# A written order of operations for the opening of an attention and mixing kernel, with 64-bit weights rounded by an integer add

## The chip, the cores and the metric

The kernel runs on one core of a Trainium2 chip. The metric is the device time of one execution in microseconds (us), lower is better. Engines: PE does matmuls (TensorE) and PEld loads their weights, DVE is VectorE, ACT is ScalarE, POOL is GpSimd, SP issues the DMAs.

## What is computed

Three layers in a row, over 4 batches of 768 tokens: local attention with 8 heads of 64, a token-mixing layer, and a gated layer. The opening of the kernel does attention and the first half of the mixing layer for batch 0:

```python
# attention, per chunk of 32 tokens: 8 memory keys and 16 + 32 + 8 keys around the chunk
a = softmax(scale * q_c @ k_full.T);  out_c = a @ v_full
# mixing layer
theta = x @ w_theta
zr, zi = x * cos(theta), x * sin(theta)
y = einsum('ts,bsd->btd', w_tok_r, zr) + einsum('ts,bsd->btd', w_tok_i, zi)
u = x + y
x2 = u + max(u @ w_ch, 0)
# gated layer: h = gelu(x2 @ w_in); u, v = halves; v normalised, mixed over tokens by w_sg, + b_sg
out = x2 + (u * v_s) @ w_out
```

`w_theta`, `w_tok`, `w_ch`, `w_in` and `w_out` come as 64-bit floats, everything else as 32-bit floats.

## The kernel before

Every product of the mixing layer is made of three fp32r matmuls: each operand is split into a high part `hi` (the value rounded to fp32r, written by ACT) and a rest `lo` (value minus `hi`, by DVE), and hi x hi, hi x lo and lo x hi are added up in PSUM.

*Attention* goes in blocks i of 128 tokens, six to a batch. `att_s` (S): 64 small matmuls give the scores, DVE takes the maximum (L255) and subtracts it (L257), ACT does exp (L261). `att_t` (T): four transposes on PE (L269), copied out by ACT (L273). `att_v` (V): 64 small matmuls (L244), DVE makes the reciprocal of the sums (L281, L284) and multiplies (L285); that is x. `att_x` (X): four transposes of x (L296), split into `xhi` (ACT, L122) and `xlo` (DVE, L123). S and V share one PSUM tile, T and X another.

*Units.* The mixing layer's work is a list of units. For batch 0 there are twelve, one for each half of the output tokens and each of six token blocks s; from unit 12 on a unit covers both halves and half of the channels. `theta(n)` is 12 matmuls (L323; 512 columns wide for batch 0, 256 later), then on DVE a rounding step to the nearest integer (L334) and a subtraction (L337), on ACT sine, absolute value and cosine, and on DVE the multiplication by x that gives z (L348). `z_split` makes the hi and lo of z. `mix_group(n, g)` is six matmuls of 384 columns (L390); the last token block adds x to the sum (L400, L401) and stores it (L402).

*Weights.* A 64-bit piece is brought to fp32 by bit operations on its two words: `bits` (ACT reads the high word, L160; DVE shifts it, L163, sets the sign, L166, and makes a power of two out of the exponent, L170). `convert` then has ACT write `hi` (L213) and DVE compute the low word's share (L214), value minus `hi` (L218) and their sum (L219). The four `w_theta` pieces and the first two of the twelve `w_tok` pieces go through `convert_pe`, which lets PE add the parts by matmuls with an identity.

*Order.* Before the loop a list of calls starts blocks 0 to 3; the loop over units then places attention steps and weight conversions by fixed distances (`s_it`, `x_it`). Within what depends on what, the framework's scheduler reorders instructions. `keep_warm` issues matmuls on a constant whose result is not used. SP issues all DMAs in program order; a load waits until its room is free.

Of the kernel before, what the change touches and what calls it, by code (L numbers as in the profile page):

```python
# [18 lines left out]
DM = H * D  # L19
# [12 lines left out]


def net_kernel(tc, qt, kw, vw, ident, w_theta, w_tok, w_ch, w_in, w_sg, w_out, g_ln, b_sg, out):
# [27 lines left out]
    st_cm, stg = opened("stg", bufs=2)  # L62
# [5 lines left out]
    id_th = stg.tile([128, 128], F32, name="id_th", bufs=1)  # L68
    id_r = stg.tile([128, 128], F32R, name="id_r", bufs=1)
    id_neg = stg.tile([128, 128], F32R, name="id_neg", bufs=1)  # L70
# [19 lines left out]
    def x_set(pool, i, xt):  # L90
        return (
            xt,
            pool.tile([128, KD, S], F32R, name=f"xhi{i}"),
            pool.tile([128, KD, S], F32R, name=f"xlo{i}"),
        )

    sets = {0: x_set(set0, 0, [set0.tile([128, DM], F32, name=f"xt{s}") for s in range(NBLK)])}
    xt_of = [sets[0][0], [None] * NBLK]
# [7 lines left out]

    def keep_warm(bank, n):

        for _ in range(n):
            nc.tensor.matmul(  # L110
                out=bank, lhsT=busy, rhs=busy.unsqueeze(1).to_broadcast([128, 4, 128]),
                start=True, stop=True,
            )
# [7 lines left out]
    def split(hi, lo, src, eng=None):  # L121
        nc.scalar.activation(out=hi, in_=src, func=AF.Copy)  # L122
        (eng or nc.vector).tensor_tensor(out=lo, in0=src, in1=r32(hi), op=ALU.subtract)  # L123

    class Weights:
# [28 lines left out]
        def bits(self, raw, n, scale, mag="act", rem="dve"):  # L154
# [4 lines left out]
            m = self.pool.tile([128, self.n], I32, tag="cvm", name="cvm", bufs=self.ncm)[:, 0:n]  # L159
            nc.scalar.activation(  # L160
                out=h.bitcast(F32), in_=high.bitcast(F32), func=AF.Copy, scale=REBIAS
            )
            nc.vector.tensor_scalar(  # L163
                out=h, in0=h, scalar1=3, scalar2=None, op0=ALU.logical_shift_left
            )
            nc.vector.scalar_tensor_tensor(  # L166
                out=h, in0=high, scalar=-0x80000000, in1=h,
                op0=ALU.bitwise_and, op1=ALU.bitwise_or,
            )
            nc.vector.tensor_scalar(  # L170
                out=m, in0=h, scalar1=-0x800000, scalar2=None, op0=ALU.bitwise_and
            )
            return high, low, h, m

        def convert_pe(self, j, scale=None, bank=None):

            if j >= len(self.pieces):
                return
            _, hi, lo = self.pieces[j]
            raw, n, _ = self.raw.pop(j)  # L180
            one = 1.0 if scale is None else scale
            high, low, h, m = self.bits(raw, n, scale)

            w, rest = h.bitcast(F32), lo
            nc.scalar.activation(out=hi, in_=w, func=AF.Copy, scale=one)
            nc.vector.scalar_tensor_tensor(
                out=rest, in0=low.bitcast(U32), scalar=one * 2.0 ** -52, in1=m.bitcast(F32),
                op0=ALU.mult, op1=ALU.mult,
            )
            step = n if n <= 512 else n // 2  # L190
            for c in range(0, n, step):
                cv = (bank or th_tile)()[:, 0:step]
                c = slice(c, c + step)
                nc.tensor.matmul(
                    out=cv, lhsT=id_sb if scale is None else id_th, rhs=w[:, c],
                    start=True, stop=False,
                )
                nc.tensor.matmul(out=cv, lhsT=id_neg, rhs=hi[:, c], start=False, stop=False)
                nc.tensor.matmul(out=cv, lhsT=id_r, rhs=rest[:, c], start=False, stop=True)
                nc.scalar.activation(out=lo[:, c], in_=cv, func=AF.Copy)  # L200

        def convert(self, j, mag="act", rem="dve", sub="dve", add="dve"):
            if j >= len(self.pieces):
                return
            eng = {"dve": nc.vector, "pool": nc.gpsimd}
            _, hi, lo = self.pieces[j]
            raw, n, wide = self.raw.pop(j)
            if not wide:
                split(hi, lo, raw[:, 0:n].bitcast(F32), eng[sub])
                return  # L210
            high, low, h, m = self.bits(raw, n, None)
            w, rest = h.bitcast(F32), m.bitcast(F32)
            nc.scalar.activation(out=hi, in_=w, func=AF.Copy)  # L213
            nc.vector.scalar_tensor_tensor(  # L214
                out=rest, in0=low.bitcast(U32), scalar=2.0 ** -52, in1=rest,
                op0=ALU.mult, op1=ALU.mult,
            )
            eng[sub].tensor_tensor(out=w, in0=w, in1=r32(hi), op=ALU.subtract)  # L218
            eng[add].tensor_tensor(out=lo, in0=w, in1=rest, op=ALU.add)  # L219
# [6 lines left out]

    def load_att(i):
        q = at.tile([128, NPAIR, 128], F32, tag="q", name="q", bufs=NQ)
        nc.sync.dma_start(out=q, in_=qt[i].rearrange("p (a t) -> p a t", a=NPAIR))
        q_t[i] = q  # L230
        nc.sync.dma_start(out=ka[i % NK], in_=kw[i])
# [3 lines left out]

# [16 lines left out]
    def att_s(i):  # L252
        sc = pairs(at2_tile(), NKEY, q_t.pop(i), ka[i % NK])
        mx = at.tile([128, 2, NPAIR], F32, tag="mx", name="mx")
        nc.vector.tensor_reduce(out=mx, in_=sc, axis=AX.X, op=ALU.max)  # L255
        p = at.tile([128, NPAIR, 2, NKEY], F32, tag="p", name="p", bufs=1)
        nc.vector.tensor_tensor(  # L257
            out=p.rearrange("p a j k -> p j a k"), in0=sc,
            in1=mx.unsqueeze(3).to_broadcast([128, 2, NPAIR, NKEY]), op=ALU.subtract,
        )  # L260
        nc.scalar.activation(out=p, in_=p, func=AF.Exp, scale=SCALE)  # L261
        p_t[i] = p

    def att_t(i, warm=0):
        p = p_t.pop(i).rearrange("p a j k -> p (a j k)")
        tp = at_tile()
        keep_warm(tp, warm)
        for a in range(NPAIR):
            nc.tensor.transpose(  # L269
                out=tp[:, 128 * a:128 * a + 128], in_=p[:, 128 * a:128 * a + 128], identity=id_sb  # L270
            )
        pt = at.tile([128, NPAIR, 128], F32, tag="pt", name="pt", bufs=1)
        nc.scalar.activation(out=pt, in_=tp.rearrange("p (a t) -> p a t", a=NPAIR), func=AF.Copy)  # L273
        pt_t[i] = pt

    def att_v(i):
        b, s = divmod(i, NBLK)
        x = xt_of[b % 2][s]
        pv = pairs(at2_tile(), D + 1, pt_t.pop(i), va[i % NKV])
        rs = at.tile([128, 2, NPAIR, 1], F32, tag="rs", name="rs")  # L280
        nc.vector.tensor_scalar(  # L281
            out=rs, in0=pv[:, :, :, D:D + 1], scalar1=1e-9, scalar2=None, op0=ALU.add
        )
        nc.vector.reciprocal(out=rs, in_=rs)  # L284
        nc.vector.tensor_tensor(  # L285
            out=x.rearrange("p (a j d) -> p j a d", a=NPAIR, j=2),
            in0=pv[:, :, :, 0:D], in1=rs.to_broadcast([128, 2, NPAIR, D]), op=ALU.mult,
        )

    def att_x(i, warm=0):  # L290
        b, s = divmod(i, NBLK)
        x, (_, xhi, xlo) = xt_of[b % 2], sets[b % 2]
        tp = at_tile()
        keep_warm(tp, warm)
# [784 lines left out]
```

## Time and profile before

| | us |
|---|---|
| median of 3 runs | 745.52 (745.11 to 746.04) |
| the profiled execution | 747.1 |
| its span, first to last instruction | 745.3 |
| PE busy in the span | 727.9 |
| DVE busy | 524.7 |
| ACT busy | 319.0 |

Busy times are unions over an engine's instructions. Matmuls are pipelined, and the end of one is modelled, so the duration that is listed for a matmul is longer than the distance to the next. The granted clock is given as a share of TensorE's full 2.4 GHz; its other level is half of that. A line number can be that of a helper (L122 and L123 are `split`).

### The profile page before, as it was taken

Reading aid. Unit: us, or ns where it says so; the run is one execution under the profiler, and the core shown is the slowest. Engines: PE = TensorE matmul, PEld = TensorE weight load, DVE = VectorE, ACT = ScalarE, POOL = GpSimd, SP = SyncE. Lnnn points to the kernel's source line nnn. Section 1 sums busy time; section 2 is a strip of 40 time slices with the busy share of each in tenths; the row PEclk is TensorE's granted clock in tenths of the full one; section 3 lists DMA queues with packets and bytes.
Section 4 is the critical chain, followed back from the end, with each engine's and each line's share of the span. In section 5 each row is a group of like instructions: output and inputs, shape, how many; then the busy total and the mean of one; then the engine's idle time right before and its main releaser. Section 6 shows DMA issues by size and latency. Waiting matters only on the chain.

```text
span 745.3 us, 16147 instructions
## 1 busy us (share of the span) xinstructions
PE 727.9 (98%) x6958; PEld 672.3 (90%) x6958; DVE 524.7 (70%) x981; ACT 319.0 (43%) x482; POOL 0.3 (0%) x6
## 2 busy tenths in 40 slices
PE   8988999999999999999999999999999999999997
PEld 4766888989999999999999998999899989998997
DVE  5989898757657575799449967977446743774375
ACT  5867543635555455463213516622342233224320
POOL 0000000000000000000000000000000000000000
PEclk9998999999999999999999999999999999999999
DMA  9865465523334240061049936003100310030002
GB/s 350 303 212 176 157 209 165 185 73 122 98 112 127 89 157 31 33 226 69 1 172 352 306 130 246 1 1 106 65 1 1 116 54 1 1 116 11 1 1 85
DMA packets 33047, 86.89 MB, mean 117 GB/s; under 512 B 3792, under 2 KB 16208, under 8 KB 32976
## 3 DMA queue, kind: packets, MB, share of 16 engines
q1 hardware_dynamic: 32976, 85.87, 33.8%
q8 instruction: 54, 0.88, 0.5%
q14 instruction: 17, 0.14, 0.1%
HBM read 66.98 MB, written 18.87 MB: 115 GB/s over the span
## 4 chain that ended last, share of the span: by engine, by line
PE 77%; DVE 14%; ACT 5%; DMA 2%; issue 1%; SPq 0%; ACTq 0%; DVEq 0%
PE acc L390 19%; PE acc L676 13%; PE acc L444 9%; PE th L323 8%; PE acc L552 7%; PE acc L590 7%; PE att L714 6%; PE att L244 3%; DVE z L348 1%; DVE cvh L166 1%; ACT L339 1%; PE att L269 1%; PE th L714 1%; PE acc L714 1%; PE att L296 1%
## 5 line engine op out<-in xcount | busy, mean ns | idle before, releaser
L390 PE MATMUL acc<-tok,slot 128*128 128x384 f32 x552 | 116.9, 342 | 2.2 <-ACT slot L360 2.2
L390 PE MATMUL acc<-slot 128*128 128x384 f32 x552 | 115.3, 339 | 0.0
L390 PEld LDWEIGHTS acc<-tok,slot 128*128 128x128 f32 x552 | 94.5, 188 | 4.6 <-ACT slot L360 2.7
L390 PEld LDWEIGHTS acc<-slot 128*128 128x128 f32 x552 | 95.5, 188 | 1.7
L676 PE MATMUL acc<-sg_hi,vhi_all 128*128 128x384 f32 x192 | 64.6, 336 | 0.8 <-ACT vhi_all L122 0.8
L676 PE MATMUL acc<-sg_lo,vhi_all 128*128 128x384 f32 x192 | 64.4, 336 | 0.0
L676 PE MATMUL acc<-sg_hi,vlo_all 128*128 128x384 f32 x192 | 64.3, 336 | 0.0
L323 PE MATMUL th<-th_hi,xhi 128*128 128x256 f32 (+1 forms) x168 | 52.8, 314 | 1.7 <-ACT xhi L122 1.6
L323 PE MATMUL th<-th_hi,xlo 128*128 128x256 f32 (+1 forms) x168 | 51.6, 307 | 0.3 <-DVE xlo L123 0.3
L323 PE MATMUL th<-th_lo,xhi 128*128 128x256 f32 (+1 forms) x168 | 50.7, 302 | 0.0
L122 ACT ACTIVATE gop<-gv_all 128x384 fp32r<-128x384 f32 (+1 forms) x28 | 15.9, 571 | 76.7 <-DVE gv_all L685 51.6
L681 DVE SCALAR_TENSOR_TENSOR gv_all<-acc,g_col,b_bc 128x384 f32<-128x384 f32 x32 | 19.6, 614 | 41.0 <-PE acc L676 41.0
L590 PE MATMUL acc<-x3lo,in_hi 128*128 128x384 f32 x128 | 43.0, 336 | 0.0
L590 PE MATMUL acc<-x3hi,in_hi 128*128 128x384 f32 x128 | 43.0, 336 | 0.0
L590 PE MATMUL acc<-x3hi,in_lo 128*128 128x384 f32 x128 | 43.0, 336 | 0.0
L444 PE MATMUL acc<-ulo,ch_hi 128*128 128x384 f32 x128 | 42.8, 334 | 0.0
L444 PE MATMUL acc<-uhi,ch_hi 128*128 128x384 f32 x128 | 42.8, 334 | 0.0
L444 PE MATMUL acc<-uhi,ch_lo 128*128 128x384 f32 x128 | 42.8, 334 | 0.0
L559 DVE BATCH_NORM_STATS2 bn<-gv_all 128x6 f32<-128x512 f32 x24 | 16.6, 694 | 33.2 <-ACT gv_all L558 33.2
L552 PE MATMUL acc<-in_hi,x3lo 128*128 128x512 f32 x96 | 38.0, 396 | 0.0
L552 PE MATMUL acc<-in_lo,x3hi 128*128 128x512 f32 x96 | 38.0, 396 | 0.0
L552 PE MATMUL acc<-in_hi,x3hi 128*128 128x512 f32 x96 | 38.0, 395 | 0.0
(186 smaller groups left out, 1574.1 us busy)
## 6 DMA issues: line engine op xcount, KB each, us to landing
va<-vw SPq DMA_DIRECT2D x24, 520.0 KB, 3.8
ka<-kw SPq DMA_DIRECT2D x24, 512.0 KB, 4.7
raw<-w_tok SPq DMA_DIRECT2D x12, 768.0 KB, 5.3
q<-qt SPq DMA_DIRECT2D x24, 256.0 KB, 3.7
u_dram<-u SPq DMA_DIRECT2D x32, 192.0 KB, 1.9
uf<-u_dram SPq DMA_DIRECT2D x8, 768.0 KB, 6.6
x_dram<-x2e SPq DMA_DIRECT2D x32, 192.0 KB, 3.6
x3f<-x_dram SPq DMA_DIRECT2D x8, 768.0 KB, 4.9
```

What stands on the lines that cost most here:

```text
L122: nc.scalar.activation(out=hi, in_=src, func=AF.Copy)
L166: nc.vector.scalar_tensor_tensor(out=h, in0=high, scalar=-0x80000000, in1=h, op0=ALU.bitwise_and, op1=ALU.bitwise_or,)
L244: nc.tensor.matmul(out=out[32 * c:32 * c + 32, j, n * a:n * a + n], lhsT=lhs[h, a, 32 * c:32 * c + 32], rhs=rhs[h, 4 * a + c, :], start=Tr ...
L323: nc.tensor.matmul(out=th, lhsT=a[:, k, tok], rhs=w[:, k, cols], start=(i == 0), stop=(i == 3 * KD - 1),)
L390: nc.tensor.matmul(out=acc[:, 0:TC], lhsT=z[ri][:, zc], rhs=w[:, ri], start=(first and i == 0), stop=(last and i == 5),)
L444: nc.tensor.matmul(out=acc[:, 0:TC], lhsT=w[:, k, ee], rhs=x[:, k, :], start=(i == 0), stop=(i == 3 * KD - 1),)
L552: nc.tensor.matmul(out=acc, lhsT=x[:, k, tt], rhs=w[:, k, :], start=(i == 0), stop=(i == 3 * KD - 1),)
L559: nc.vector.bn_stats(out=p3["bn"][s], in_=gv)
L590: nc.tensor.matmul(out=acc[:, 0:TC], lhsT=w[:, k, ff], rhs=x[:, k, :], start=(i == 0), stop=(i == 3 * KD - 1),)
L676: nc.tensor.matmul(out=acc[:, 0:TC], lhsT=v, rhs=w, start=(i == 0), stop=(i == 3 * NBLK - 1))
L681: nc.vector.scalar_tensor_tensor(out=g, in0=acc[:, 0:TC], scalar=p3["g"][:, f:f + 1], in1=p3["b"][:, tt], op0=ALU.mult, op1=ALU.add,)
L714: nc.tensor.matmul(out=bank, lhsT=wt[:, k, ee], rhs=xt[:, k, :], start=(fresh and i == 0), stop=(i == 5), skip_group_check=not fresh,)
```

## The change

The opening, up to the theta step of unit 13, is written as one list of words, `OPENING`, worked off under `tc.manual_schedule()`, in which the instructions of each engine stay in the order of the list. A word names one operation of one engine and its numbers: S, m, p, e, T, t, V, r, x, X, h, l are attention's steps, A.n.k a quarter (later a half) of theta's matmuls, `ac`, `af`, `as`, `aa`, `ak`, `z` the steps to z, `zh` and `zl` its split, M a mix group, `u` and `us` the addition and the store, `th`- and `tk`-words the seven steps of a conversion of `w_theta` or `w_tok`, `wt` and `wm` the loads of the pieces, W.n n warm-up matmuls. The rest of the loop begins at unit 12 and is scheduled as before.

Three operations change. (1) A 64-bit weight is rounded by an integer add: ACT reads the low word scaled to the range 0 to 8 into an integer (L906), DVE adds it to the shifted bits (L925), and the piece is then split like any value; no piece uses PE. This holds for `w_ch`, `w_in` and `w_out` too. (2) Theta's rounding step is done by ACT, which adds the magic number while it copies out of PSUM (L375); DVE does the rest in one operation (L380). This holds for all units. (3) The hi and lo of the second x set lie in three rooms of the raw pieces of `w_tok` and in one of the conversion's, instead of in a pool that is opened when the conversion's pool is closed.

```diff
+OPENING = """
+k.0 wt.1 q.0 id wt.0 wt.3 k.1 v.0 v.1 q.1 wt.2 wm.0 wm.1 thH.1 wm.4 ths.1 thR.1 thg.1 W.16 S.0 tha.1
...
+"""
...
+    def x_tile(b, j, h):
+        if (b % 2, j, h) not in sets:
+            tag = "cv0" if j and h else "raw"
+            t = sta.tile([128, 4 * TC], F32R, tag=tag, name=tag, bufs=1 if j and h else NRAW1)
...
+    def single(high, low, h, r):
+        nc.scalar.activation(
+            out=h.bitcast(F32), in_=high.bitcast(F32), func=AF.Copy, scale=REBIAS
+        )
+        nc.scalar.activation(out=r, in_=low.bitcast(U32), func=AF.Copy, scale=2.0 ** -29)
+        nc.vector.tensor_scalar(
+            out=h, in0=h, scalar1=3, scalar2=None, op0=ALU.logical_shift_left
+        )
+        nc.vector.scalar_tensor_tensor(
+            out=h, in0=high, scalar=-0x80000000, in1=h, op0=ALU.bitwise_and, op1=ALU.bitwise_or
+        )
+        nc.vector.tensor_tensor(out=h, in0=h, in1=r, op=ALU.add)
+        return h.bitcast(F32)
...
-            nc.vector.scalar_tensor_tensor(
-                out=rest, in0=low.bitcast(U32), scalar=2.0 ** -52, in1=rest,
-                op0=ALU.mult, op1=ALU.mult,
-            )
...
-            eng[sub].tensor_tensor(out=w, in0=w, in1=r32(hi), op=ALU.subtract)
-            eng[add].tensor_tensor(out=lo, in0=w, in1=rest, op=ALU.add)
...
-        nc.vector.tensor_scalar(
-            out=t, in0=th, scalar1=MAGIC, scalar2=MAGIC, op0=ALU.add, op1=ALU.subtract
-        )
-        nc.vector.tensor_tensor(out=t, in0=th, in1=t, op=ALU.subtract)
...
+        nc.scalar.activation(out=t, in_=tmp["th", n], func=AF.Copy, bias=MAGIC)
...
+        nc.vector.scalar_tensor_tensor(
+            out=t, in0=t, scalar=MAGIC, in1=tmp.pop(("th", n)), op0=ALU.subtract, op1=ALU.subtract
+        )
...
+        with tc.manual_schedule():
+            for word in OPENING.split():
+                name, *at_ = word.split(".")
+                step[name](*map(int, at_))
+        close(sb_cm)
+        for it in range(NFIRST, NU):
```

How the instructions stand, first on DVE in the middle of the opening, before: weight pieces 3 and 4 (`cvh`, `cvm`) between attention (`att`, `mx`, `p`, `xlo`) and theta (`th`, `t`).

```order
L166 SCALAR_TENSOR_TENSOR cvh<-raw,cvh 128x768
L257 TENSOR_TENSOR p<-att_609,mx 128x2x4x64
L123 TENSOR_TENSOR xlo_122<-att,xhi_121 128x4x128
L170 TENSOR_SCALAR cvm<-cvh 128x768
L163 TENSOR_SCALAR cvh<-cvh 128x768
L214 SCALAR_TENSOR_TENSOR cvm<-raw,cvm 128x768
L255 TENSOR_REDUCE mx<-att_671 128x8
L218 TENSOR_TENSOR cvh<-cvh,tok_3_109 128x768
L257 TENSOR_TENSOR p<-att_671,mx 128x2x4x64
L334 TENSOR_SCALAR t<-th 128x512
L219 TENSOR_TENSOR tok_3_110<-cvh,cvm 128x768
```

And after, also on DVE, one whole piece (number 4, in tile `cv_710`) between attention, theta (L380), and the split of a z (L446).

```order
L912 TENSOR_SCALAR cv_710<-cv_710 128x768
L254 TENSOR_REDUCE mx<-att_714 128x8
L380 SCALAR_TENSOR_TENSOR t<-t,th 128x512
L259 TENSOR_TENSOR p<-att_714,mx 128x2x4x64
L324 TENSOR_TENSOR xlo_116<-att,xhi_115 128x4x128
L446 TENSOR_TENSOR slot<-z,slot 128x512
L918 SCALAR_TENSOR_TENSOR cv_710<-raw,cv_710 128x768
L446 TENSOR_TENSOR slot_x<-z,slot 128x512
L925 ISA cv_710<-cv_710 128x1536
L411 TENSOR_TENSOR z<-z,xt_119 128x1024
L949 TENSOR_TENSOR tok_4_112<-cv_710,tok_4_111 128x768
```

A piece has four operations instead of six; the add (L925) is issued as an instruction over half-words, 1536 for 768 words.

On PE, late in the opening, before: V of block 7 (`va`), T of block 8 (`p`), mix groups, S of block 9 (`ka`).

```order
L390 MATMUL acc<-slot 128x384 x5
L390 MATMUL acc<-slot,slot_x 128x384
L244 MATMUL att_1479<-va_126,pt 32x65 x32
L269 MATMUL att<-id_sb,p 128x128 x4
L390 MATMUL acc<-slot 128x384 x5
L390 MATMUL acc<-slot,slot_x 128x384
L390 MATMUL acc<-slot 128x384 x5
L390 MATMUL acc<-slot,slot_x 128x384
L244 MATMUL att_1545<-ka_124,q 32x64 x32
```

And after, V of block 7, a mix group, S of block 8, X of block 7.

```order
L273 MATMUL att<-id_sb,p 128x128 x4
L466 MATMUL acc<-slot 128x384 x5
L466 MATMUL acc<-slot,slot_x 128x384
L241 MATMUL att_1386<-va_126,pt 32x65 x32
L466 MATMUL acc<-slot 128x384 x5
L466 MATMUL acc<-slot,slot_x 128x384
L241 MATMUL att_1433<-ka_123,q 32x64 x32
L311 MATMUL att<-id_sb,slot_x 128x128 x4
```

Between a V and the S that takes over its PSUM tile stood two mix groups and a T in this place; now one mix group stands there.

## Rows read from the trace of the kernel before

**Rows 1.** Stretches: length, then busy (instructions) PE, PEld, DVE, ACT, POOL; clock; DMA
```profile
0.00:38.60 38.60, 36.34 (x447) 22.15 (x448) 28.63 (x50) 25.69 (x41) 0.33 (x6) 1.00 0.84 316
38.60:57.50 18.90, 15.42 (x341) 12.07 (x346) 17.14 (x29) 13.15 (x18) 0.00 (x0) 1.00 0.66 224
57.50:65.00 7.50, 6.08 (x78) 4.52 (x63) 6.43 (x9) 5.69 (x8) 0.00 (x0) 0.54 0.64 216
65.00:141.90 76.90, 73.62 (x1245) 64.67 (x1244) 70.15 (x121) 39.15 (x55) 0.00 (x0) 1.00 0.55 175
141.90:745.30 603.40, 596.41 (x4877) 568.92 (x4876) 402.34 (x774) 235.28 (x364) 0.00 (x0) 1.00 0.27 92
```
**Rows 2.** Timeline of PE, end of the opening: start us, us, engine, line, operation
```profile
138.81 1.03 PE L390 MATMUL acc<-slot 128*128 128x384 f32 x5
139.68 0.34 PE L390 MATMUL acc<-slot,slot_x 128*128 128x384 f32 x1
139.86 0.60 PE L296 MATMUL att<-id_sb,slot_x 128*128 128x128 f32 x4
140.21 1.31 PE L390 MATMUL acc<-tok,slot 128*128 128x384 f32 x6
...
141.89 0.86 PE L244 MATMUL att<-ka,q 64*32 64x64 f32 x64
142.68 0.80 PE L390 MATMUL acc<-slot 128*128 128x384 f32 x3
...
144.60 0.69 PE L390 MATMUL acc<-slot 128*128 128x384 f32 x3
```
**Rows 3.** Timeline of ACT and PE, the first 40 us
```profile
7.22 0.68 ACT L160 ACTIVATE cvh<-slot 128x512 f32<-128x512 f32 x1 [5.22 <-DMA slot<-w_theta]
...
20.95 0.39 PE L323 MATMUL th<-th_hi,xhi 128*128 128x512 f32 x1
...
23.52 0.40 PE L323 MATMUL th<-th_hi,xlo 128*128 128x512 f32 x1
...
35.95 0.34 PE L390 MATMUL acc<-tok,slot 128*128 128x384 f32 x1
...
39.52 0.34 PE L390 MATMUL acc<-tok,slot 128*128 128x384 f32 x1
```
**Rows 4.** PE's waits after 142 us: us in total, times, longest
```profile
PE att L296 <- DVE slot_x L285: 0.9, 2, 0.5
...
PE acc L676 <- ACT vhi_all L122: 0.8, 1, 0.8
```
**Rows 5.** Groups of DVE, 0 to 142 us: busy us, mean ns of one, idle before
```profile
L166 DVE SCALAR_TENSOR_TENSOR cvh<-raw,cvh 128x768 int32<-128x768 int32 x12 | 11.4, 952 | 0.1
...
L348 DVE TENSOR_TENSOR z<-z,xt 128x1024 f32<-128x1024 f32 x6 | 7.3, 1222 | 5.5 <-ACT z L347 5.5
...
L163 DVE TENSOR_SCALAR cvh<-cvh 128x768 int32<-128x768 int32 x12 | 6.5, 550 | 0.1
...
L334 DVE TENSOR_SCALAR t<-th 128x512 f32<-128x512 f32 x6 | 4.1, 680 | 1.8 <-PE th L323 1.7
...
L186 DVE SCALAR_TENSOR_TENSOR th_lo<-slot,cvm 128x512 fp32r<-128x512 uint32 x4 | 2.8, 692 | 0.1
...
L284 DVE RECIPROCAL rs<-rs 128x8 f32<-128x8 f32 x12 | 2.4, 198 | 0.1
...
L163 DVE TENSOR_SCALAR cvh<-cvh 128x512 int32<-128x512 int32 x4 | 1.7, 421 | 0.6 <-ACT cvh L160 0.6
...
L795 DVE MEMSET busy<- 128x128 bf16 x1 | 0.2, 165 | 0.8 <-PEq L1065 0.8
```
**Rows 6.** Groups of ACT in the same stretch
```profile
L160 ACT ACTIVATE cvh<-raw 128x768 f32<-128x768 f32 x12 | 10.9, 908 | 6.3 <-DVE slot L219 4.5 <-DVE tok L219 1.8
L339 ACT ACT_TABLE_LOAD x6 | 7.7, 1283 | 0.1
```
**Rows 7.** DMA issues by line: size each, median us from issue to landing
```profile
raw<-w_tok SPq DMA_DIRECT2D x12, 768.0 KB, 5.3
```

More of the change, by code (lines that the diff above doesn't have):

```diff
@@ L1 @@
+import functools
 import math
@@ L190, in convert_pe @@
[L190 to L206, printed above, removed]
             raw, n, wide = self.raw.pop(j)
             if not wide:
-                split(hi, lo, raw[:, 0:n].bitcast(F32), eng[sub])
+                split(hi, lo, raw[:, 0:n].bitcast(F32))
                 return
-            high, low, h, m = self.bits(raw, n, None)
-            w, rest = h.bitcast(F32), m.bitcast(F32)
-            nc.scalar.activation(out=hi, in_=w, func=AF.Copy)
+            w = self.single(j, raw, n)
@@ L874, in net_kernel, with load_id, load_th, load_tok @@
-        z_split(0)
-        att(att_s, 2)
-        theta(1)
-        tok_conv()
-        att(att_t, 2)
-        att(att_v, 2)
-        z_split(1)
-        att(att_s, 3)
-        for it in range(NU):
+        def load_id():
+            nc.sync.dma_start(out=id_sb, in_=ident)
+        raws = {}
+        def load_th(k):
+            raws["th", k] = slot(3 * 512, "slot", I32)
+            nc.sync.dma_start(out=raws["th", k][:, 0:2 * DM], in_=w_theta[k].bitcast(I32))
+        def load_tok(j):
+            raws["tk", j] = sta.tile([128, 4 * TC], I32, tag="raw", name="raw", bufs=NRAW1)
+            nc.sync.dma_start(out=raws["tk", j], in_=w_tok[j % NBLK, j // NBLK].bitcast(I32))
@@ new lines, in conv_lo, with warm @@
+        def conv_lo(w, j):
+            f = conv_tile(w, j, 0).bitcast(F32)
+            hi, lo = tmp.pop(("c", w, j))
+            if w == "th":
+                nc.vector.scalar_tensor_tensor(
+                    out=lo, in0=f, scalar=1.0 / TWO_PI, in1=r32(hi), op0=ALU.mult, op1=ALU.subtract
+                )
+            else:
+                nc.vector.tensor_tensor(out=lo, in0=f, in1=r32(hi), op=ALU.subtract)
+        def warm(n):
+            bank = acc_tile()
+            for _ in range(n):
+                nc.tensor.matmul(
+                    out=bank, lhsT=busy, rhs=busy.unsqueeze(1).to_broadcast([128, 4, 128]),
+                    start=True, stop=True,
+                )
@@ new lines, in net_kernel @@
+        for w in ("th", "tk"):
+            for n, f in (
+                ("H", conv_h), ("R", conv_r), ("s", conv_shift), ("g", conv_sign),
+                ("a", conv_round), ("h", conv_hi), ("l", conv_lo),
+            ):
+                step[w + n] = functools.partial(f, w)
+        nc.vector.memset(busy, 1.0)
+        with tc.manual_schedule():
[3 more added lines that the diff above has]
+        close(sb_cm)
@@ L912, in net_kernel @@
                 split_u(0)
-        close(s1_cm)
+        close(sa_cm)
         close(wk_cm)
```

441 lines of the change are left out of this document (240 added, 201 removed).

## Prediction

> **What bounds the kernel now.** I first read the stretches of the span [rows 1]. PE is busy almost everywhere, but busy says little here: a 384-column matmul is listed with 0.34 us, while five of them start in 0.87 us [rows 2], one every 0.174 us, so two are always in flight. I therefore count PE work by spacing, not by duration. By the same reading a group of 64 small attention matmuls (S or V) costs 0.79 us, four transposes (T or X) 0.35 [rows 2], a 512-column theta matmul 0.234 (eleven in 2.57 us) [rows 3] and a 256-column one half of that.
>
> Next, the place up to which the two programs do the same work. The rewritten opening ends with the theta matmuls of unit 13. In the kernel before these end at 144.60 us; by then PE has also done one X, one S and nine matmuls of unit 12 (0.35 + 0.79 + 9 x 0.174 = 2.7) [rows 2], which the rewritten opening leaves for later. So the opening takes 144.6 - 2.7 = **141.9 us** now.
>
> What must PE do in it? 12 S and 12 V (19.0), 12 T and 8 X (7.0), 72 theta matmuls of 512 columns (16.8), 24 of 256 (2.8) and 48 groups of six mix matmuls (50.1): 95.7 us. So 46 us of the opening go to waiting, to warm-up matmuls and to the identity matmuls of six weight conversions. After 141.9 us the largest things that PE waits for are one operand of the transposes, 0.9 us in all, and 0.8 us once in the last stage [rows 4]. What the change can win lies ahead of 141.9 us.
>
> There DVE holds the end: it works 17.14 of 18.90 us, 6.43 of 7.50 and 70.15 of 76.90 in the stretches after 38.6 us [rows 1], and PE waits for it. In the stretch from 57.5 us the granted clock is 0.54, that is, PE is at 1.2 GHz for most of it after having stood idle; that is a consequence of the waiting.
>
> **The change part by part.** *Weights.* One 768-wide piece costs DVE two one-source operations (0.55 each) and four two-source operations (0.95) [rows 5] now: 4.9 us. Afterwards: one shift 0.55, sign 0.95, the integer add, the subtraction 0.95. I take 0.95 for the add, the row of a two-source operation over as many words; bounds below. That is 3.4 us, or 1.5 less on ten pieces (15.0). Two pieces that now use PE go from 3.0 to 3.4 (+0.8), and four 512-wide ones from 2.23 to 2.49 (+1.0; 0.42 and 0.69 each [rows 5]). *Theta.* The rounding operation leaves DVE for ACT: six times 0.68 [rows 5] and two half as wide, 4.9 in all. DVE is relieved by 15.0 - 0.8 - 1.0 + 4.9 = 18.1 us by rows. The 33 rows of DVE up to 142 us, of which the first and last and six between are shown [rows 5], add up to 135.8 us, and DVE was busy 122.4 (28.6 + 17.1 + 6.4 + 70.2 [rows 1]), a ratio of 0.90, since operations that do not depend on each other overlap; so some 16 us of busy time. *ACT* gets twelve reads of the low words at 0.91 [rows 6], four narrower ones and eight rounding steps, and loses the copies out of the identity matmuls and three of its twelve reloads of function tables (1.28 each [rows 6]): about 9 us more than the 84 us it has now. *PE* loses the identity matmuls; 38 warm-up matmuls become 50. I cost these at nothing: each run of them stands before a matmul that waits for DVE anyway. Without that cover the 11 behind the first theta step would cost 11 x 0.234 = 2.6 us.
>
> *The order.* Each engine now works off its queue in the written order. I add up DVE's queue. Its first conversion waits for one transfer less than now; ACT begins it at 7.22 us now [rows 3] and would at about 6.5, so DVE starts at 7.2. Up to the multiplication of unit 1's z (close to the first mix group) there are 30 operations at 0.69, four at 0.42, three pairs at 0.3 (the reciprocal's 0.20 and a smaller one), two at 0.55, six at 0.95 and two at 1.22: 32.5 us [rows 5]. So the first mix group starts at about **39 us**; now it starts at 35.95 [rows 3], but with theta for unit 2 still ahead. From there to the last half of unit 5's z: 26 at 0.69, six at 0.55, sixteen at 0.95, four at 0.3, four at 1.22: 42.5 us. The last half of unit 5's z would then be there at 7.2 + 75.0 = 82.2 us with every duration paid in full, at 7.2 + 0.90 x 75.0 = 74.7 us with the overlap of today and no wait at all. ACT has about 39 us of work in the same second stretch (twelve reads at 0.91 and three reloads at 1.28 [rows 6], 35 others most of which are like the 0.68 of [rows 3]), so they will wait for each other; I take **80 us**.
>
> Behind it PE has 30 mix groups, 5 S, 5 V, 5 T, 2 X and the two theta units: 31.3 + 7.9 + 2.5 + 2.8 = 44.5 us. In it I see two kinds of wait. S stands one mix group (1.04 us) behind V but needs V's result taken out by DVE, about 1.25 us later with handovers: 0.2 to 0.7 us, four times, 1.8. And weight piece 10, which is loaded last because its room comes free last, needs 5.3 us to land [rows 7] and some 5 us of ACT and DVE, against 9.7 us of PE work between: 0.7. So the opening ends at 80 + 0.3 + 44.5 + 2.5 = **127.3 us**, 14.6 earlier. The bounds: 74.7 + 44.5 = 119 and 82.2 + 0.3 + 44.5 + 4 = 131.
>
> *The add* is an instruction that the trace does not have: the built program issues it over 1536 elements of half a word for 768 words. Bounds from rows: not less than the fast one-source row, 0.55; not more than 1536 elements at the slope between the 768-wide row (0.95) and the 1024-wide one (1.22) [rows 5], 1.76. I take 0.95, since each step would then read one word of each source, as the two-source rows do. The Trainium skill, VectorE: DVE Perf Modes, section "What auto-detection actually checks", says that a two-source operation goes to two elements per cycle where every tensor is 16-bit with step one: estimated from that page's 0.96 GHz, 768 cycles and its fixed 150 cycles, 0.96 us, which leaves the sum as it is; without a program for that mode it would be one element per cycle, the half-word rival below. Its table "Specifications" says that integer operands are converted to fp32 and exact only below 2^24, which speaks against adding bit patterns with the ordinary operation; no run here shows either.
>
> *After the opening.* The rounding step of 36 more theta units moves to ACT, which has much idle time (235 of 603 us busy [rows 1]); mix groups use a z two units after its theta, so nothing is late. Twenty more weight pieces lose two DVE operations each beside a PE without gaps, so nothing there either, but four of them (w_out) lie right before the 0.8 us for which PE waits in the last stage [rows 4], and I count 0.75 won. The second x set in raw rooms, the stores and the loads cost nothing that I can see, apart from piece 10.
>
> **Sum.** 14.6 + 0.75 = 15.35 us. The profiled execution takes 747.1 us, its span 745.3 and 1.8 around it; that becomes 731.7. The median of the runs is 745.52, 1.6 lower; it becomes 730.2, and I say **730**.
>
> **The rivals.**
>
> *The add takes one half-word per step.* Then it costs 1.76 and, 512 words wide, 1.22: 0.81 more eight times and 0.53 more four times before unit 5's z is done, 8.6 us: 739 (737 to 741). For it: no row of such an operation. Against: nothing in the rows either, only that reading.
>
> *The written order starves PE as today's does.* Now PE stands at 39.5 us [rows 3] with 14.4 us of its 95.7 done and needs 102.4 for the other 81.3: it loses 21. If the new opening loses as much behind its first mix group (79.3 left at about 39), it ends at 139.5: 743 (740 to 745). For it: DVE, ACT and PE queues are full and strict, one late operation holds all behind it. Against: DVE has 16 us less to do, and theta and attention of the next units stand between the mix groups.
>
> *Slower: the add is far slower than any DVE row.* Twelve of them lie ahead of unit 5's z; they eat 15.35 us when each costs 1.28 more, so from about 2.2 us for 768 words on. At 3 us it is 755. For it: an instruction of its own kind, of unknown speed. Against: every DVE row here fits about 0.15 us and 1.05 ns per element.
>
> *Better:* DVE keeps its overlap and never waits: 119 to 121 us, 722 to 724, and below.
>
> **How the numbers follow.** Forecast (722 to 736) 0.70; add at half-words 0.13; starved order 0.08; below 722 0.04; slower 0.05. The range takes the forecast and both dear cases up to 740: 722 to 740. 0.2% is 1.5 us, about what a measurement of this kernel can tell from no change: faster is all but the slow case and half of the starved one, 0.90; same 0.05; slower 0.05.
>
> **What would show it.** Right: the first mix group at 38 to 41 us; the last half of unit 5's z near 80; theta of unit 13 done near 127; the add at 0.95; granted clock 1.00 from 50 to 70 us; no change between then and the last stage. Wrong: the add above 1.5; PE waits of over 1 us behind 80 us; weight piece 10 more than 2 us late; or a PE that waits for ACT in the stretch to 80 us, since then ACT, not DVE, is the engine that I should have summed.

## The result, and the profile after

The changed kernel takes **737.48 us** (median of 4 runs, 736.6 to 738.01), the kernel before 745.78 (745.11 to 746.7): ratio 0.9887, 95% interval 0.987 to 0.9904. That is 8.3 us faster, inside the range and a little over half of the 15.4 that were forecast. Between the two profiled executions the gain is 10.5 us (747.1 to 736.6, spans 745.3 to 734.8); the profile before was 1.3 above its median and the one after 0.9 below, so 2.2 of the 10.5 are in no median.

The opening of the changed kernel, by stretches (us, then busy time of each engine with its instruction count, granted clock, DMA share, GB/s); the cuts are the first mix group (41.87), the last half of unit 5's z (81.94) and the end of theta 13 (129.38):

```profile
0.00:41.90 41.90, 34.30 (x563) 20.00 (x563) 30.03 (x51) 26.68 (x40) 0.33 (x6) 0.96 0.85 318
41.90:81.90 40.00, 38.27 (x622) 32.93 (x621) 38.99 (x62) 37.28 (x52) 0.00 (x0) 1.00 0.70 231
81.90:129.40 47.50, 47.24 (x871) 42.82 (x870) 38.25 (x67) 22.82 (x32) 0.00 (x0) 1.00 0.59 187
```

In the middle stretch DVE works 38.99 of 40.00 us; behind it PE has almost no gap. In [rows 1] DVE was less full (70.15 of 76.90). The groups of DVE in the same opening, to be read beside [rows 5]:

```profile
L918 DVE SCALAR_TENSOR_TENSOR cv<-raw,cv 128x768 int32<-128x768 int32 x12 | 11.4, 952 | 0.1
L925 DVE CUSTOM_DVE_ANT_0 cv<-cv 128x1536 uint16<-128x1536 uint16 x12 | 11.3, 953 | 0.4
L925 DVE CUSTOM_DVE_ANT_0 cv<-cv 128x1024 uint16<-128x1024 uint16 x4 | 2.8, 690 | 0.4
L912 DVE TENSOR_SCALAR cv<-cv 128x768 int32<-128x768 int32 x12 | 6.6, 554 | 2.0 <-ACT cv L900 2.0
```

The integer add costs 953 ns for 768 words, the same as the two-source row beside it. What PE waited for up to 129.4 us (total, times, longest):

```profile
PE att L241 <- issue: 2.8, 2, 2.6
PE att L273 <- ACT p L267: 2.4, 3, 0.9
PE acc L954 <- DVE busy L975: 1.0, 1, 1.0
PE att L241 <- DVE xt L300: 0.8, 1, 0.8
PE att L241 <- ACT pt L280: 0.7, 2, 0.4
PE th L362 <- DVE xlo L324: 0.7, 1, 0.7
```

The largest is one that no other engine ends: "issue". PE's timeline shows it in the middle of the S of block 1, of which 55 matmuls run at 15.01 and the other nine at 18.35:

```profile
15.01 0.77 PE L241 MATMUL att<-ka,q 64*32 64x64 f32 x55 [0.81 <-DVE xt L300]
18.35 0.32 PE L241 MATMUL att<-ka,q 64*32 64x64 f32 x9 [2.58 <-issue]
```

DVE's longest wait between 7 and 42 us is for that S:

```profile
DVE mx L254 <- PE att L241: 3.2, 1, 3.2
```

From 129.4 us to the end PE waits for three things (against [rows 4]): the transposes' operands still cost 0.9 and 0.9, and the 0.8 of the last stage is gone.

```profile
PE att L311 <- DVE xt L300: 0.9, 2, 0.5
PE att L311 <- DVE slot_x L300: 0.9, 2, 0.5
PE att L792 <- DVE o L806: 0.7, 1, 0.7
```

### The profile page after: what moved, and what is told of

It reads as the page before. It is cut to its first block, busy times and chain, and to the rows that moved or that the text cites. A ratio compares the mean times of both kernels' runs of the same rounds, so it can differ in the third digit from the quotient of the medians.

```text
span 734.8 us, 16088 instructions
## 1 busy us (share of the span) xinstructions
PE 719.0 (98%) x6938; PEld 666.3 (91%) x6938; DVE 484.4 (66%) x879; ACT 347.2 (47%) x547; POOL 0.3 (0%) x6
## 4 chain that ended last, share of the span: by engine, by line
PE 80%; DVE 11%; ACT 3%; DMA 3%; issue 1%; SPq 0%; DVEq 0%; ACTq 0%
PE acc L466 22%; PE acc L754 13%; PE acc L539 9%; PE th L362 7%; PE acc L647 7%; PE acc L685 7%; PE att L792 6%; PE att L241 3%; DMA gop<-w_out 1%; PE att L311 1%; PE th L792 1%; PE acc L792 1%; DVE cv L918 1%; PE att L273 1%; DMA raw<-w_tok 1%
## 5 line engine op out<-in xcount | busy, mean ns | idle before, releaser
L759 DVE SCALAR_TENSOR_TENSOR gv_all<-acc,g_col,b_bc 128x384 f32<-128x384 f32 x32 | 19.7, 614 | 43.1 <-PE acc L754 43.1
L433 ACT ACTIVATE slot<-z 128x512 fp32r<-128x512 f32 (+1 forms) x42 | 29.1, 692 | 24.2 <-DVE z L411 23.9
L380 DVE SCALAR_TENSOR_TENSOR slot_x<-slot_x,th 128x256 f32<-128x256 f32 x34 | 14.3, 420 | 39.7 <-ACT slot_x L375 39.5
L754 PEld LDWEIGHTS acc<-sg_hi,vhi_all 128*128 128x128 f32 x192 | 36.0, 188 | 0.5 <-ACT vhi_all L144 0.5
```

What stands on the lines that cost most here:

```text
L433: nc.scalar.activation(out=hi, in_=sc_t[n], func=AF.Copy)
L754: nc.tensor.matmul(out=acc[:, 0:TC], lhsT=v, rhs=w, start=(i == 0), stop=(i == 3 * NBLK - 1))
L759: nc.vector.scalar_tensor_tensor(out=g, in0=acc[:, 0:TC], scalar=p3["g"][:, f:f + 1], in1=p3["b"][:, tt], op0=ALU.mult, op1=ALU.add,)
```

## A ruler for the runs

Names in the list stand for different matmuls in the two programs, so I compare them where both have done the same: at the 313th mix matmul (147.56 us before, 137.39 after; at it theta of unit 14, two X (eight matmuls) and one S are done as well). From 157 us of the changed kernel to its first channel matmul (368.66) the two traces keep the same distance, 10.08 to 10.09 us. PE's work is counted by the spacings of the prediction; what is left of the time is lost (warm-up and identity matmuls, all of which stand before the first mix group, count as lost). Read from the timelines, in us:

| kernel | median (ratio to before) | first mix group | unit 5's z done | 313th mix matmul | lost before / behind the first mix group |
|---|---|---|---|---|---|
| before | 745.78 | 35.95 | 92.02 | 147.56 | 25.0 / 19.8 |
| changed | 737.48 (0.9887) | 41.87 | 81.94 | 137.39 | 25.5 / 9.1 |
| e0_again | 738.80 (0.9897) | 40.95 | 82.36 | 138.42 | 24.5 / 11.1 |
| e4_free_order | 746.67 (1.0006) | 34.68 | 88.87 | 146.14 | 22.6 / 20.8 |
| e5_add_alone | 747.49 (1.0017) | 32.03 | 87.75 | 147.46 | 21.1 / 23.6 |
| e9_old_ops | 759.54 (1.0179) | 43.61 | 92.20 | 157.07 | 27.2 / 27.1 |
| e3_round_dve | 741.94 (0.9937) | 44.04 | 86.59 | 143.62 | 27.6 / 13.2 |
| e1_few_warm | 736.43 (0.9853) | 40.45 | 80.59 | 137.58 | 24.0 / 10.7 |
| e6_f32_warm | 737.08 (0.9869) | 38.99 | 80.20 | 137.67 | 22.6 / 12.3 |
| e8_two_fixes | 737.58 (0.9877) | 39.05 | 79.41 | 138.62 | 22.6 / 13.2 |
| e2_late_loads | 737.77 (0.9885) | 42.29 | 83.03 | 138.63 | 25.9 / 10.0 |
| e7_loads_after_s1 | 739.52 (0.9900) | 42.66 | 83.63 | 139.13 | 26.3 / 10.1 |
| e10_few_late_warm | 737.84 (0.9889) | 41.88 | 82.17 | 138.25 | 25.5 / 10.0 |
| e11_quiet_dma | 738.65 (0.9883) | 43.29 | 83.68 | 139.15 | 26.9 / 9.5 |

Half widths of the intervals are 0.001 to 0.0024. Behind the first mix group most of the difference between before and changed lies ahead of unit 5's z: PE loses 13.5 us up to it before and 4.7 after, with DVE busy 49.7 of 56.1 us and 39.1 of 40.1. From there to the 313th mix matmul it loses 6.3 and 4.6.

The changed kernel itself, run again, shows how far one profile carries:

> The changed kernel once more, as the ruler for the others. In its first profile PE stands 2.58 us in the middle of the second S (attention step of unit 1), after 449 matmuls and weight loads, for no releaser; the first mix group starts at 41.87 us, the last half of unit 5's z is done at 81.94, theta of unit 13 at 129.38, the span is 734.8. If the stall belongs to the program: all of it again, landmarks within 0.5 us, stall 2 to 3 us, time 737 to 738. If it was an accident of that execution: no stall, first mix group near 39, span near 732.

The stall came again (2.19 us), the opening a microsecond later, and 2 us were lost at a place where the first profile loses nothing: theta of a late unit waits for DVE, whose part of the rounding (L380) stands behind a split and a weight conversion.

```profile
321.22 1.21 PE L466 MATMUL acc<-slot 128*128 128x384 f32 x6
324.04 0.39 PE L362 MATMUL th<-th_hi,raw 128*128 128x256 f32 x1 [1.61 <-DVE slot_x L380]
```

In e1 PE waits for the same step there, 0.8 us; in the profiles of before and of the changed kernel it does not. The prediction put the later units' rounding at nothing, and these two runs show that it can cost up to 2 us. So landmarks of a single profile are good to about 1 us, the span to about 2.

## Which part of the change gives the gain

My theory: DVE holds the end of the opening, the change takes 16 us of busy time from it, and most of that comes out. The rival: the order is what matters. Three runs take the parts asunder.

**The order left to the scheduler** (same list, same operations; what the scheduler makes of it is not the order of before):

```diff
-        with tc.manual_schedule():
+        if True:
```

> The changed kernel with the same operations, but the opening's list is left to the scheduler, which reorders it on PE, DVE and ACT; the integer add, the rounding on ACT and the raw rooms stay. It parts what the written order gives from what fewer DVE operations give. Mine: DVE's sum decides, the order only lets PE work behind it; of the 8.1 us (medians) fewer operations give about half, so 741 to 743, with the opening's first 96 theta matmuls done at 133 to 136 us. Rival A, the order gives nothing beyond the scheduler's: 737 to 739. Rival B, the order gives all: 745 to 747.

Nothing is left of the gain: 1.0006, interval 0.9996 to 1.0016, against the 741 to 743 that I expected. **The new weights alone, in the kernel before:**

```diff
-            high, low, h, m = self.bits(raw, n, None)
...
+            nc.scalar.activation(out=r, in_=low.bitcast(U32), func=AF.Copy, scale=2.0 ** -29)
...
+            nc.vector.tensor_tensor(out=h, in0=h, in1=r, op=ALU.add)
...
         def convert_pe(self, j, scale=None, bank=None):
+            self.convert(j, scale=scale)
```

> The kernel before with one part of the change: every weight piece goes the new way (low word read by ACT, integer add on DVE, no identity matmuls); the order stays the scheduler's, theta's rounding stays on DVE. Eight 768-wide pieces of the opening save 1.5 us of DVE each, two cost 0.4 more, four 512-wide ones 0.26 more: 10 us by rows ahead of unit 13. Mine: half or more of it arrives, since DVE was busy for 93 of 100 us behind 38.6: 738 to 742. Rival: PE and ACT (nine more microseconds of reads on ACT) take it back: 744 to 747.

Nothing again (1.0017, 1.0 to 1.0034). The first mix group does come 3.9 us earlier and unit 5's z 4.3, and by the 313th mix matmul all of it is gone. **The written order with the old operations:**

```diff
         def conv_round(w, j):
-            nc.vector.tensor_tensor(out=h, in0=h, in1=conv_tile(w, j, 1), op=ALU.add)
+            nc.vector.tensor_scalar(
+                out=m, in0=h, scalar1=-0x800000, scalar2=None, op0=ALU.bitwise_and
+            )
+            nc.vector.scalar_tensor_tensor(
+                out=m.bitcast(F32), in0=words(w, j, 0).bitcast(U32), scalar=one * 2.0 ** -52,
+                in1=m.bitcast(F32), op0=ALU.mult, op1=ALU.mult,
+            )
...
+            nc.vector.tensor_tensor(out=lo, in0=f, in1=conv_tile(w, j, 1).bitcast(F32), op=ALU.add)
```

> The written order with the old operations: in the opening each weight piece takes six DVE operations again (mask, product with the low word, difference, sum in place of the integer add and one difference), ACT reads no low words; theta's rounding stays on ACT. Up to the last z half of unit 5 that is 1.1 us of DVE more for each of four theta pieces and 1.5 for each of eight mixing pieces, 16.4 us. The operations alone gave nothing under the scheduler's order (0.9 earlier up to equal work with all of them, nothing with the add alone). Theory: in the written order DVE's sum decides, so all of it comes back: first mix group at 48 to 50 us, unit 5's z at 96 to 99, the first 96 theta matmuls done at 147 to 150, 753 to 757 us, slower than the kernel before. Rival, the order is the whole gain and DVE has slack in it as it had under the scheduler: unit 5's z at 85 to 90, 738 to 743.

759.54 us, 12.8 slower than the kernel before. (Theta's rounding on ACT and the raw rooms stay in this run.) So fewer operations under the scheduler's order are worth nothing, the written order with six operations a piece costs 13 us, and together they are worth 8. This run is not the kernel before in another order, though: six pieces whose parts PE added before (the four of `w_theta` and two of `w_tok`) took four DVE operations there and take six here, by the rows of 0.69 and 0.95 us an estimated 9 us more for DVE. What the order is worth with exactly the old operations is not shown. Nor is it DVE's sum alone that comes back: of 16.4 us by rows unit 5's z shows 10.3, the 313th mix matmul 19.7.

The stretch from 7 us to the end of unit 5's z shows why; one row each of before, the free order, the old operations and the changed kernel, columns as above (the third busy time is DVE's, the fourth ACT's):

```profile
7.00:92.02 85.02, 77.55 (x1078) 58.03 (x1076) 76.28 (x125) 58.08 (x84) 0.00 (x0) 0.96 0.67 238
```
```profile
7.00:88.87 81.87, 71.10 (x1178) 55.15 (x1176) 68.50 (x110) 70.36 (x96) 0.00 (x0) 0.94 0.72 258
```
```profile
7.00:92.20 85.20, 69.20 (x1167) 52.11 (x1154) 82.66 (x132) 55.10 (x78) 0.00 (x0) 0.96 0.68 239
```
```profile
7.00:81.94 74.94, 66.66 (x1166) 50.70 (x1145) 68.33 (x110) 61.48 (x89) 0.00 (x0) 0.98 0.78 278
```

In the written order DVE idles 2.5 us (old operations) or 6.6, of which 3.2 are its wait for the stalled S; there its sum sets the pace. In the scheduler's order it idles 8.7 before, and 13.4 once the operations are fewer: 68.50 busy, as in the changed kernel, but spread over 81.87. What DVE is spared becomes waiting, since it, ACT and PE wait for each other in turn. PE's waits of that run up to 140 us:

```profile
PE th L362 <- ACT xhi L321: 3.1, 2, 2.7
PE att L241 <- DVE xt L300: 3.1, 1, 3.1
PE att L273 <- ACT p L267: 2.4, 3, 1.5
PE att L311 <- DVE xt L300: 2.0, 1, 2.0
```

And in an order written for four DVE operations a piece, filled with six, PE waits right where the list expects DVE to be done, up to 3.2 us at a time, also behind unit 5's z. The first of these rows belongs to it: its three S each begin 0.1 us after DVE's multiplication for x (L300) ends.

```profile
PE att L241 <- issue: 4.2, 3, 2.2
PE acc L466 <- DVE slot L954: 3.5, 2, 2.9
PE att L273 <- DVE raw L324: 3.2, 1, 3.2
PE acc L466 <- DVE tok L954: 2.0, 2, 1.3
```

**DVE's price in the written order**, from six operations of 0.68 us put back:

```diff
-        nc.scalar.activation(out=t, in_=tmp["th", n], func=AF.Copy, bias=MAGIC)
+        if n < NBLK:
+            nc.vector.tensor_scalar(out=t, in0=tmp["th", n], scalar1=MAGIC, scalar2=None, op0=ALU.add)
+        else:
+            nc.scalar.activation(out=t, in_=tmp["th", n], func=AF.Copy, bias=MAGIC)
```

> Theta's rounding step goes back from ACT to DVE for units 0 to 5 of the opening (six 512-column steps, 0.68 us each); the other units keep it on ACT. Theory, DVE's queue holds the end of unit 5's z: two steps lie ahead of the first mix group (1.4 later, 43.2), six ahead of unit 5's z (4.1 later, 86.0), and theta of unit 13 comes at 132.5 to 133.5; time 740.5 to 742. Rival, ACT or PE holds it and DVE has slack: under 1 us, time 737 to 738.5.

Unit 5's z came 4.2 to 4.7 us later for 4.1 of work, and the time rose by 3.1 against the changed kernel beside it. In this order the theory of DVE's sum holds for these six operations; under the scheduler's, where e4 and e5 took more than that from DVE, nothing came of it.

**The 11 warm-ups behind the first theta step** (of a line of the list only the words around the change are shown, here and below):

```diff
-W.4 A.0.2
+A.0.2
...
-af.0 W.4 T.2
+af.0 T.2
...
-m.3 W.3 A.2.0
+m.3 A.2.0
```

> The 11 warm-up matmuls behind the first theta step are left out. If waits for DVE cover them, as the prediction has it: first mix group and the end of theta 13 within 0.5 us of the changed kernel (41 to 42, 129.4 to 130.5), 737 to 739. If they stand in PE's way: 2.6 us (11 times 0.234) earlier, 735. If they hold the clock: granted clock under 0.9 somewhere from 25 to 40 us, first mix group after 43, 739 to 742.

First mix group at 41.88, no change in time: covered, as the prediction had it.

## The stop at PE's 451st instruction

The trace records the blocks in which PE's instructions arrive as a queue of its own, `q8 instruction: 54, 0.88` (packets, MB): 16 KB each. In the changed kernel the first of them begins to arrive at 15.92 us, when 449 instructions of PE have run (matmuls, weight loads and the few semaphore events that the trace has), and the 451st is the first matmul behind the stop. The block has landed at 17.00, and PE goes on at 18.35. All ten runs in which PE stops here go on 1.2 to 1.5 us after that landing; in the other four (before, e1, e4, e9) the block had landed 2.7 us or more before PE came to this instruction. That ties the stop to the block more closely than the count does. Behind it the clock falls too: 0.91 of full speed is granted from 15 to 20 us and 0.87 from 20 to 30.

```profile
15.00:20.00 5.00, 2.41 (x71) 1.60 (x72) 1.74 (x3) 1.88 (x4) 0.00 (x0) 0.91 1.00 407
20.00:30.00 10.00, 9.74 (x160) 5.70 (x158) 8.28 (x16) 7.29 (x12) 0.00 (x0) 0.87 0.81 291
```

Three runs try to move the stop. With fewer warm-ups:

```diff
-thg.0 W.10 T.0 thR.3
+thg.0 W.2 T.0 thR.3
...
-thg.3 W.4 V.0 thl.0
+thg.3 V.0 thl.0
...
-tha.3 W.4 S.1
+tha.3 S.1
```

> Sixteen of the 34 warm-up matmuls ahead of the second S are left out (10 become 2, two runs of 4 go), 32 instructions fewer on PE ahead of it; nothing else changes. Theory: PE runs out of fetched instructions at its 449th and the next block of them comes late; with 32 fewer ahead, the second S ends at about instruction 430 and does not stall: stall 0, first mix group 38.5 to 39.5 (2.6 to 3.2 earlier, since DVE waited 3.2 us for that S), theta of unit 13 done at 126 to 127, time 734 to 735. Rival A, the stall is tied to a time (15.6 to 18.3 us) and not to a count: it stays, on whatever PE does then, and the time stays at 737 to 738. Rival B, the 2.6 us are given back (DVE or the transfers hold the first mix group anyway): stall gone, first mix group still at 41 to 42, time 737. Rival C, the warm-ups did keep the clock up: granted clock under 0.9 from 15 to 30 us, and half of the gain or more lost.

With three loads later:

```diff
-wt.2 wm.0 wm.1 thH.1 wm.4 ths.1
+wt.2 thH.1 ths.1
...
-thl.0 v.2 r.0
+thl.0 v.2 wm.0 wm.1 wm.4 r.0
```

> All warm-ups stay; the first three loads of mixing weights (768 KB each) are issued after the third load of v, behind the first V, instead of in one row with the first loads. Theory: the block of instructions waits behind these loads, since the DMA engines are busy without a gap from 3 to 24 us; with 2.3 MB less ahead of it, it starts to arrive before 15 us (15.92 now) and the stall is under 0.5 us; first mix group 38.5 to 40, time 734 to 735.5. Rival: the block is asked for by count and arrives no earlier: stall 2 to 3 us as before, time 737 to 738. Third: the late weights are themselves late, ACT waits over 2 us for the first mixing piece, and the first mix group comes after 42 us.

With warm-ups on fp32, 4, 3 and 1 in place of 16, 10 and 4 or 5:

```diff
-    busy = const.tile([128, 128], BF16, name="busy")
+    busy = const.tile([128, 128], F32, name="busy")
```

> The changed kernel with warm-up matmuls on fp32 operands: 13 in place of 50, each meant to hold PE as long as four of the bf16 ones (four passes: S, fp32 with 64 columns on eight tiles, takes 12.3 ns a matmul), so that PE stays as busy with 50 fewer instructions ahead of the second S (two to a warm-up). If running out of fetched instructions at number 449 is what stalls that S, and the clock is what spoiled the run with few warm-ups: no stall in S, granted clock 1.00 from 11 to 20 us (0.50 in the run with few warm-ups from 11 us on), first mix group at 38.5 to 39.5, unit 5's z at 79 to 80, time 734 to 736. If the stall is tied to the time of 15.6 to 18.3 us: stall of 2 us or more, first mix group at 41 to 42, 737 to 739. If the fp32 matmul is not four times as long: gaps of PE ahead of the first T and V, and the clock at 0.5 from 11 us on, 736 to 738.

With fewer warm-ups (e1) the stop is gone, but PE idles 2.74 us ahead of the first T and the clock falls to 1.2 GHz for most of the next 11 us (0.54 granted); with fp32 warm-ups it stays at 2.4. The same stretch of e1 and of e6:

```profile
11.00:22.00 11.00, 8.57 (x151) 5.71 (x149) 8.71 (x16) 5.07 (x10) 0.00 (x0) 0.54 1.02 411
```
```profile
11.00:22.00 11.00, 9.31 (x219) 5.45 (x217) 9.29 (x19) 6.78 (x13) 0.00 (x0) 1.00 1.02 409
```

An fp32 warm-up is recorded as two matmuls that start 0.43 us apart at full clock, not as one of four times 0.22, so there are 32 instructions fewer ahead of the second S, not 50. In e6 the stop is down to 0.86 us and stands in a theta step, again ahead of the 451st instruction: it goes with the count and not with the place in the program. The first mix group comes at 38.99, as forecast for the changed kernel. In e2 the DMA engines stayed full, the block came at 16.33 and the stop was 2.85 us, so that run says nothing on the loads. The next one (e7) places the same loads behind the end of that S:

```diff
-wt.2 wm.0 wm.1 thH.1 wm.4 ths.1
+wt.2 thH.1 ths.1
...
-S.1 thh.3 k.3 m.1
+S.1 thh.3 k.3 wm.1 wm.0 wm.4 m.1
```

> The run with late loads held the DMA engines as full as before (1.00 to 1.06 of their time from 9 to 20 us), since the loads began just as the block of instructions was asked for. Here the three loads of mixing weights stand behind the fourth load of k, which waits for the second S to end, so that the DMA engines run empty at about 13 to 16 us; all 50 warm-ups stay. If the block waits for the DMA engines: it starts to arrive by 14.5 us (15.5 to 16.3 in all runs so far), the second S stalls under 0.5 us, the first mix group comes at 38.5 to 40 unless its weights are late (ACT's first read of a mixing piece is at 23.6 now; the load lands at about 19). 734 to 737. If it does not: stall 2 to 3 us at instruction 449, 737 to 739.

The engines were full to 16 us all the same (0.94 of the time from 16 to 17), the block came at 15.94, the stop was 2.57 us: nothing new. The last one (e11) places every load that the second S does not need behind the first V:

```diff
-k.1 v.0 v.1 q.1 wt.2 wm.0 wm.1 thH.1 wm.4 ths.1
+k.1 q.1 v.0 thH.1 ths.1
...
-thl.0 v.2 r.0
+thl.0 v.2 wt.2 v.1 wm.1 k.2 q.2 wm.0 wm.4 r.0
```

> The changed kernel with all 50 warm-ups, and with every load that is not needed before the second S issued behind the third load of v, which waits for the first V (13.2 us): 3.6 MB ahead of that point instead of 6.9, so that the DMA engines run empty between about 11.5 and 13.5 us, the time at which PE passes its 200th instruction. PE has stopped at its 450th or 451st instruction in every run of this list that was not held up before it, wherever that instruction stood (the second S, or a theta step with fp32 warm-ups). If the next block of instructions waits behind the loads: it starts to arrive by 13 us (15.5 to 16.3 in those runs), no stop in the second S, first mix group at 38.5 to 40, unit 5's z at 79 to 80.5, 735 to 737 (weight piece 10 then holds unit 10's mix group at about 117). If the block does not wait for the loads: it comes at 15.5 to 16.3 again, the stop is 2 to 3 us, 737 to 739. If the loads themselves are late: waits of ACT for them of over 1 us, first mix group behind 41.

In e11 the engines did run empty, the block came at 14.11, and S stopped behind the same 55 matmuls for 0.38 us only; but a theta weight was 3.9 us late, and PE waited 3.1 us ahead of its first theta step. So with the loads out of the way the block came 1.8 us earlier than in the changed kernel, not the 3 that were expected.

```profile
15.18 0.77 PE L241 MATMUL att<-ka,q 64*32 64x64 f32 x55 [0.30 <-issue]
16.33 0.32 PE L241 MATMUL att<-ka,q 64*32 64x64 f32 x9 [0.38 <-issue]
```
```profile
12.00:14.00 2.00, 1.32 (x67) 0.83 (x66) 1.97 (x5) 0.99 (x2) 0.00 (x0) 1.00 0.03 10
```

**Where the 2.9 us go that e6 wins early.** At unit 5's z 1.7 of them are left. At 109 us PE is still 1.8 ahead of the changed kernel; then it stops for 1.8, ahead of its 3522nd instruction, 3071 or some 12 times 256 behind the first stop. Weight piece 10, for which ACT waits, lands in the same moment:

```profile
111.46 0.51 PE L466 MATMUL acc<-slot 128*128 128x384 f32 x2 [1.81 <-issue]
111.65 0.90 ACT L900 ACTIVATE cv<-raw 128x768 f32<-128x768 f32 x1 [5.71 <-DMA raw<-w_tok]
```

e8 moves two words in e6's list:

```diff
-V.9 wm.10 r.9 v.11 M.8.2
-x.9 S.10 q.12 m.10 M.9.2 k.12 p.10 tkH.10 M.8.3 e.10 tks.10
+V.9 wm.10 r.9 M.8.2
+x.9 S.10 q.12 m.10 M.9.2 k.12 v.11 p.10 M.8.3 e.10 tkH.10 tks.10
```

> The run with fp32 warm-ups, and in the list two words moved: ACT's exponential of unit 10 ahead of the first read of weight piece 10, and the load of v for unit 11 behind the load of k for unit 12. In the run with fp32 warm-ups PE was 1.8 us ahead of the changed kernel at 109 us and lost it in a stop of 1.8 us at 111.5 with no releaser, as a block of its instructions began to arrive only at 109.1, behind the load of piece 10 and two others; then the transposes of unit 10 waited 0.7 for that exponential. If these two took the gain: no stop over 0.5 us behind 100 us, the first 96 theta matmuls done at 128.5 to 130 on PE's count (130.9 in that run), 734.5 to 736.5. Rival: weight piece 10 itself holds the tenth unit's mix group (it lands at 111.6 in both runs): that group at 117 as before, 736 to 738.

The wait for the exponential is gone, the stop at the 3522nd instruction stays (2.02 us), and the time is that of e6. It lies in the rival's range, but not for the rival's reason: in e8 ACT reads piece 10 at 110.58, before PE goes on at 110.89, and unit 10's mix group (117.05 in the changed kernel, 117.29 in e6, 118.26 in e8) has no idle time of PE ahead of it in any of the three. In e8 the clock falls behind the stop, to 0.50 from 112 to 115 us. No version beats the changed kernel beyond doubt: e1 is 2.4 us below its second measurement on the same chip, with intervals that do not meet (0.9831 to 0.9874, 0.988 to 0.9914), but the interval of its first (0.987 to 0.9904) overlaps with e1's; e6 and e8 overlap with both.

## Why the prediction was right in direction and nearly twice too large

*Right.* The add: 953 ns taken as 0.95, 690 for the 512-wide pieces; the half-word rival and the slow one fall with these rows. From the page that the prediction names (the Trainium skill, VectorE: DVE Perf Modes, "What auto-detection actually checks") 0.96 us was estimated, and the trace agrees (0.953). The remark against the slow rival, that every DVE row fits about 0.15 us and 1.05 ns per element, was a misreading: one-source rows do not (0.55 us for 768 words [rows 5]). DVE's queue: unit 5's z at 81.94 between 74.7 and 82.2, near the bound without overlap. The clock is 1.00 from 41.9 us on. From unit 5's z it is 47.4 us to the end of theta 13, forecast 47.3; weight piece 10 on time; no wait of PE over 1 us behind 80 us; in these two profiles the rest of the kernel unchanged up to the last stage. That 47.4 is so near is in part luck: 2.5 us of the forecast were waits of S and for piece 10, and PE's listed waits there come to 0.2; the 3.7 us that PE loses in the stretch are in steps too short to be listed.

*Sizes that were off*, in the order of the sum (15.35 forecast, 10.5 between the profiles):

- **The boundary.** The theta that ends at 144.60 [rows 2] is that of unit 14, not 13: it ends with PE's 108th theta matmul, and units 0 to 5, 12 and 13 have 96, the last of which starts at 135.98. Its 12 matmuls (1.4 us) were work done ahead that I did not take off. The opening took 140.5, not 141.9: 1.4.

```profile
135.98 0.28 PE L323 MATMUL th<-th_hi,xlo 128*128 128x256 f32 x1
144.48 0.28 PE L323 MATMUL th<-th_hi,xlo 128*128 128x256 f32 x1
```

- **The first mix group** came at 41.87, not 39. DVE's 32.5 us were right, but it waited 3.2 for the S in which PE stopped. Theta 13 ends 2.1 late (129.4 for 127.3). The stop is not shown to be the cause of all of that: e6, with a stop of 0.86 us, has the first mix group at 38.99 and unit 5's z at 80.20, both as forecast, and yet ends theta 13 at 129.65.
- **The handover.** From 129.38 to the 313th mix matmul PE needs 8.0 us for 7.1 of work by spacings; before it needed 7.1 (from 140.5 to 147.56). That is 0.9; e0, e1, e2 and e6 need 8.0 as well.
- **The last stage** gave 0.4 of 0.75, although the wait itself is gone.

These make 4.8 of 4.85, of which the last is within the play of one profile. The other 2.2 to the medians lie in the two profiles.

*The step that failed* is one that the sum did not need and the argument did: "There DVE holds the end". Behind 38.6 us DVE was busy 94 of 103 us in the kernel before [rows 1], and yet sparing it 10 us (e5), or all that the change spares it with ACT doing its share (e4), gains nothing. The rival "the written order starves PE as today's does" named the right mechanism with the wrong sign: starving is what the scheduler's order does, with the old operations and with the new (20.8 lost in e4, 23.6 in e5), and the written order ends about half of it (19.8 us lost behind the first mix group before, 9.1 after). That needs the fewer operations: with six a piece (e9) 27.1 are lost.

## What to carry to other kernels

An engine that is busy 90% of a stretch is not yet the one that sets its time: take work off it in the order that stands, and look whether the end moves, before a gain is put down to it. An order written by hand fits the durations for which it was written; try the parts of such a change alone, since here fewer operations were worth nothing without the order, and the order with six operations a piece cost 13 us. For places in two programs count matmuls, not names, and expect 1 us of play in every landmark of one profile.

## What was not expected of the hardware

PE can run out of instructions. It stopped ahead of its 451st recorded instruction in nine runs in which it reached it early, wherever that stood, and ahead of the 450th in e5; in e6 and e8 again 3071 instructions later, and in the second profile of the changed kernel 256 and 1535 later (0.8 and 0.9 us). Each of these stops ended 1.2 to 1.5 us after a block had landed. The Trainium skill, Runtime: NRT & Kernel Launch, section "Instruction fetch mechanics", says that instructions come in blocks of 16 KiB (256 instructions) while the block before runs, mostly hidden, and that PE holds 2048. The trace agrees on the blocks (0.88 MB in 54), but not on the rest: the stop cost 2.58 us, and a stop by the 451st would fit room for two blocks (512) if the trace leaves out some 60 instructions of PE, which no run here shows. Why the first block begins to arrive at 14 to 16 us in most runs and at 11.25 and 11.77 in e9 and e4, where the DMA engines were as full, stays open.

A warm-up matmul on fp32 operands was recorded as two, 0.43 us apart at full clock, against one every 0.22 us in bf16: PE is held as long with half the instructions.
